# A transformer block on one core: early loads on one queue, the first tile of x in halves, a shorter warm-up

## The chip, the cores and the metric

The kernel runs on one core of a Trainium2 chip. Such a core has a matrix engine (TensorE, PE in the profile, with its weight loads shown as PEld), a vector engine (VectorE, DVE), an engine for activations and copies (ScalarE, ACT), a general engine (GpSimd, POOL), and a queue engine (SyncE, SP) that here only issues transfers. Each engine works through its own instructions in order and waits on semaphores for the others. Operands lie in SBUF, products land in PSUM, which has eight banks of 128 x 512 numbers in fp32. The metric is the device time of one launch in microseconds.

## The reference

One transformer block on 2048 positions of width 512, all in fp32:

```python
h  = x + attention(layernorm(x), wqkv, wo)   # 32 heads of 16; position s sees s, s-2, ..., s-14
h2 = h + mlp(layernorm(h), w1, b1, w2, b2)   # 1792 wide, relu squared
# attention: q, k, v = layernorm(x) @ wqkv; logits of 8 positions per query, softmax, weighted sum of v; @ wo
```

## The kernel before

The 2048 positions are 16 tiles of 128 rows. Even and odd positions are kept apart, so that the dilated window of a query is a run of neighbours. TensorE multiplies in a rounded format (F32R); to keep accuracy each operand is split into a high and a low part, and a product is three: high by high, low by high, high by low (`mm3`, L213). The high part is a copy that rounds, on ScalarE (`hi`, L137); the low part is the difference, on VectorE or GpSimd (`lo`, L140).

The stages are these.
- Head (L675 to L722): the identity for transposes is built, x tiles 0 to 3 and the first three sets of wqkv columns are asked for, TensorE runs `WARM` transposes of the identity that nobody reads (L689), and tile 0 of x is prepared.
- First phase, tiles 0 to 3 (L723): 16 steps, four sets of columns (pairs of head groups) by four tiles. While tile t is multiplied by set 0, tile t + 1 is transposed in the middle of that product (`start_T`, L692).
- First phase, tiles 4 to 15 (`first_phase`, L752): two tiles at a time by three blocks of 512 columns. Beside it run attention for what is ready, and near its end the output product and the transposes of the first four tiles for the MLP.
- MLP, four groups of four tiles (L829), with the rest of attention beside the first ones.

q, k and v go out to DRAM and come back as windows. Attention is a stream of VectorE and GpSimd work, handed out bit by bit (`pump`, L405) by planned costs of VectorE and TensorE; chores with due times are kept in `due` and `late` (L99). All of this only decides, while the program is written, in which order the instructions stand on each engine.

Preparing a tile of x takes: the load; its statistics on VectorE (`norm_stats`, L145: L149 and L150); on GpSimd an addition and a power for one over the root of the variance (L155, L157); the normalisation on VectorE, in place (L187); four transposes on TensorE into a PSUM bank (L196); the high part on ScalarE, the low part on VectorE (both shown as L138 and L141, tiles xh and xl). A set of weights comes in four blocks of 128 rows; each is loaded (wraw), its high part goes to big_h on ScalarE, its low part to big_l.

PSUM banks are given out by turns. A turn counts its tiles and takes the next bank of its list; whoever takes a bank waits until what was in it has been read:

```python
turn = {"mm": Turn("mm0", "mm1"), "tr": Turn("tr0", "tr1")}            # L134
turn["mm"] = Turn("mm0", "mm1", "acc0", "acc1")                        # L447, first phase
turn["tr"] = turn["mm"] = Turn("mm0", "mm1")                           # L828, MLP
```

A `Turn` adds one to its count before it takes a bank, so a new one starts with its second bank. In the first phase "mm" serves the products and the transposes for the MLP (`h_T`, L606), "tr" the warm-up and the other transposes. ScalarE empties a product's bank a step later (`evac`, L483, the copy at L489).

Early in the kernel before, x 0 and x 1, two weight blocks of set 0, x 2, x 3 and all further sets are issued by the sync queue, and the first two blocks of set 0 by ScalarE's queue. VectorE's order at the head is: statistics of tile 0, of tile 1, normalisation of tile 0, low part of block 0, normalisation of tile 1, low part of tile 0, low part of block 1, statistics of tile 2. GpSimd's: L155 and L157 for tile 0, for tile 1, the fills of `zero` and `mask`, low parts of blocks 2 and 3, then L155 and L157 for tile 2. ScalarE copies the four high parts of the weights and then that of tile 0.

Of the kernel before, what the change touches and what calls it, by code (L numbers as in the profile page):

```python
# [9 lines left out]
F32R = mybir.dt.float32r  # L10
AF = mybir.ActivationFunctionType
ALU = mybir.AluOpType
X = mybir.AxisListType.X

S, D, H, DH, W, F = 2048, 512, 32, 16, 8, 1792
P = 128
KB = D // P
# [25 lines left out]
UP = 14, 14, 15, 15  # L43
HOLD = 1.0
XS = 6
WARM = 24


@with_exitstack
def block_kernel(ctx, tc, x, wqkv, wo, w1, b1, w2, b2, out):  # L50
    nc = tc.nc
# [26 lines left out]
    ident = const.tile([P, P], F32, name="ident")  # L78
# [14 lines left out]
    def row(name, shape=(P, D), dt=F32):  # L93
        return work.tile(list(shape), dt, name=name, tag="row", bufs=ROWS)
# [4 lines left out]
    due = {}  # L99
    late = {}  # L100
    now = {"slot": 0, "pe": 0.0, "dve": 0.0, "sub": -1}

    def at(delta, fn, *a):
        due.setdefault(now["slot"] + delta, []).append((fn, a))

    def after(delta, fn, *a):
        late.setdefault(now["slot"] + delta, []).append((fn, a))
# [8 lines left out]
    def run(chores):  # L116
        todo = chores.get(now["slot"], [])
        while todo:
            fn, a = todo.pop(0)
            fn(*a)  # L120

    def dve(t):
        now["dve"] += t
# [10 lines left out]
    turn = {"mm": Turn("mm0", "mm1"), "tr": Turn("tr0", "tr1")}  # L134


    def hi(dst, src):  # L137
        nc.scalar.copy(dst, src)  # L138

    def lo(eng, dst, src, h):  # L140
        eng.tensor_tensor(out=dst, in0=src, in1=h, op=ALU.subtract)  # L141

    stats = {}

    def norm_stats(key, src, delay=True):  # L145
        st = small.tile([P, 6], F32, name="st")
        mv = small.tile([P, 2], F32, name="mv", bufs=4)
        rs = small.tile([P, 2], F32, name="rs", bufs=4)
        nc.vector.bn_stats(st, src)  # L149
        nc.vector.bn_aggr(mv, st)  # L150
        dve(0.93)
        stats[key] = mv, rs

        def finish():
            nc.gpsimd.tensor_scalar(out=rs[:, 1:2], in0=mv[:, 1:2], scalar1=EPS, scalar2=None,  # L155
                                    op0=ALU.add)
            nc.gpsimd.tensor_tensor(out=rs[:, 0:1], in0=rs[:, 1:2], in1=mhalf, op=ALU.pow)  # L157
            if delay:
                nc.gpsimd.tensor_scalar(out=rs[:, 1:2], in0=mv[:, 0:1], scalar1=rs[:, 0:1],
                                        scalar2=-1.0, op0=ALU.mult, op1=ALU.mult)  # L160
        if delay:
            after(0, finish)
        else:
            finish()

    def act_stats(key, src):

        nm = small.tile([P, 2], F32, name="nm", bufs=3)
        sq = small.tile([P, 1], F32, name="sq", bufs=3)
        rs = small.tile([P, 2], F32, name="rs", bufs=4)  # L170
        scrap = row("scrap")
        nc.scalar.activation(scrap, src, AF.Identity, accum_out=nm[:, 0:1])
        nc.scalar.activation(nm[:, 1:2], nm[:, 0:1], AF.Identity, scale=-1.0 / D)
        nc.scalar.activation(scrap, src, AF.Square, bias=nm[:, 1:2], accum_out=sq)
        stats[key] = nm, rs

        def finish():
            nc.gpsimd.tensor_scalar(out=rs[:, 1:2], in0=sq, scalar1=1.0 / D, scalar2=EPS,
                                    op0=ALU.mult, op1=ALU.add)
            nc.gpsimd.tensor_tensor(out=rs[:, 0:1], in0=rs[:, 1:2], in1=mhalf, op=ALU.pow)  # L180
            nc.gpsimd.tensor_tensor(out=rs[:, 1:2], in0=nm[:, 1:2], in1=rs[:, 0:1], op=ALU.mult)
        after(0, finish)

    def norm_apply(key, dst, src, eng):
        mv, rs = stats.pop(key)
        if eng is nc.vector:
            nc.vector.tensor_scalar(out=dst, in0=src, scalar1=mv[:, 0:1], scalar2=rs[:, 0:1],  # L187
                                    op0=ALU.subtract, op1=ALU.mult)
            dve(0.46)
        else:  # L190
            nc.scalar.activation(dst, src, AF.Identity, scale=rs[:, 0:1], bias=rs[:, 1:2])

    def transposes(src, banks="tr"):
        tr = turn[banks].tile("tr").rearrange("p (k c) -> p k c", k=KB)
        for k in range(KB):
            nc.tensor.transpose(tr[:, k, :], src[:, k * P:(k + 1) * P], ident)  # L196
        now["pe"] += 0.44
        return tr
# [223 lines left out]
    xt, xT = {}, {}  # L422

    def load_x(t):
        b, r = divmod(t, 8)
        e, i = divmod(r, 4)
        xt[t] = row("xt")
        nc.sync.dma_start(xt[t], x_v[b, e, i])

    def x_stats(t):  # L430
        if t < XS:
            norm_stats(t, xt[t], t >= R)
        else:
            act_stats(t, xt[t])

    def x_norm(t):
        norm_apply(t, xt[t], xt[t], nc.scalar if t >= R else nc.vector)

    def x_T(t):
        tr = transposes(xt.pop(t))  # L440
        xT[t] = row("xh", (P, KB, P), F32R), row("xl", (P, KB, P), F32R)
        at(0, hi_T, tr, [xT[t][0]])
        after(0, lo_T, tr, [xT[t][0]], [xT[t][1]])
# [8 lines left out]
    def pair(w, k, gp):  # L452
        return w[:, k].rearrange("p (c n) -> p c n", c=3)[:, :, gp * GP:(gp + 1) * GP]
# [62 lines left out]
    def load_wqkv(gp, ks=range(KB), eng=nc.sync):  # L516
        for k in ks:
            if k % 2 == 0:
                tag = "pr" if (gp, k) in ((1, 2), (2, 0), (2, 2)) else "o"
                raws[gp] = att.tile([P, 2, D], F32, name="wraw", tag=tag, bufs=3)  # L520
            r = raws[gp, k] = raws[gp][:, k % 2, :3 * GP].rearrange("p (c n) -> p c n", c=3)
            src = wqkv[k * P:(k + 1) * P].rearrange("p (c n) -> p c n", c=3)
            eng.dma_start(r, src[:, :, gp * GP:(gp + 1) * GP])

    def hi_wqkv(gp, k):
        hi(pair(wq_h, k, gp), raws[gp, k])

    def lo_wqkv(gp, k, eng=nc.vector):
        lo(eng, pair(wq_l, k, gp), raws.pop((gp, k)), pair(wq_h, k, gp))
        if eng is nc.vector:  # L530
            dve(0.48)
# [144 lines left out]
    nc.gpsimd.memset(mhalf, -0.5)  # L676

    load_x(0)
    load_wqkv(0, (0, 1), nc.scalar)
    load_x(1)  # L680
    load_wqkv(0, (2, 3))
    for x0 in (2, 3):
        load_x(x0)
    load_wqkv(1)
# [3 lines left out]
    warm = turn["tr"].tile("tr").rearrange("p (k c) -> p k c", k=KB)  # L688
    for n in range(WARM):  # L689
        nc.tensor.transpose(warm[:, n % KB, :], ident, ident)  # L690
# [6 lines left out]
    def consts():  # L697
        nc.sync.dma_start(b1_sb, b1.rearrange("(f p) -> p f", p=P))
        nc.sync.dma_start(b2_sb, bass.AP(tensor=b2.tensor, offset=b2.offset, ap=[[0, P], [1, D]]))

    x_stats(0)
    x_stats(1)
    x_norm(0)
    hi_wqkv(0, 0)
    lo_wqkv(0, 0)
    x_norm(1)
    nc.gpsimd.memset(zero, 0.0)
    nc.gpsimd.memset(mask, 0.0)
    nc.gpsimd.affine_select(out=mask, in_=mask, pattern=[[1, R], [1, W]], base=1 - W,
                            channel_multiplier=R, compare_op=ALU.is_ge, fill=NEG)  # L710
    nc.sync.dma_start(chain(0, 0, 0, 0, [[GC, PAD], [CS, 6 * G], [1, GC]]),
                      zero.unsqueeze(1).to_broadcast([PAD, 6 * G, GC]))
    for k in range(1, 4):
        hi_wqkv(0, k)
    x_T(0)
    run(due)
    run(late)
    lo_wqkv(0, 1)
    lo_wqkv(0, 2, nc.gpsimd)
    lo_wqkv(0, 3, nc.gpsimd)  # L720
    x_stats(2)
    now["dve"] = now["pe"] = 0.0  # L722
    for n in range(16):  # L723
# [105 lines left out]
    for u in range(R):  # L829
# [9 lines left out]
        todo, halves = {}, {}  # L839
# [48 lines left out]
    h = hs[S // P - 1]  # L888
# [34 lines left out]
```

## Time and profile before

| | us |
|---|---|
| median of 3 runs | 519.74 |
| lowest and highest | 519.19, 520.53 |
| the profiled execution, whole | 518.92 |
| its span from first to last instruction | 517.1 |
| PE busy | 509.9 (99%) |
| DVE busy | 356.0 (69%) |
| POOL busy | 308.2 (60%) |
| ACT busy | 241.9 (47%) |

The span leaves out what lies around the first and the last instruction, 1.8 us here. A row of the timeline gives the start and the length in us, the engine, the line of the kernel, the operation, what it writes and reads by the program's names, shapes, and how many instructions were merged into the row; in brackets stands for how long the engine had been idle and what released it. A row of the waits gives who waited for whom, the total in us, how often, and the longest. A row of the windows gives the stretch and its length, the busy time of each engine, the granted clock, the busy share of the transfer engines and the GB/s moved. Matmul records overlap, because their ends are modelled; the distance between starts is what tells their rate.

### The profile page before, as it was taken

What the parts mean: (1) busy time and instruction counts of PE and PEld (TensorE: products, weight loads), DVE (VectorE), ACT (ScalarE), POOL (GpSimd) and SP (SyncE); (2) the same over time, 40 slices, a digit from 0 to 9 for tenths busy, and PEclk for the clock granted to TensorE, in tenths of its full rate; (3) what the DMA queues carried; (4) which work ended last, traced back from release to release, by engine and by line L of the source; (5) the groups of instructions that cost most, each with busy time, mean ns of one, the idle gap of its engine ahead of it and who ended that gap; (6) DMA issues with size and microseconds to landing.
All of it is one profiled execution on the core that took longest, in us unless ns stands there. A gap on an engine that the chain in (4) does not pass through costs nothing.

```text
span 517.1 us, 7168 instructions
## 1 busy us (share of the span) xinstructions
PE 509.9 (99%) x2385; PEld 426.1 (82%) x2385; DVE 356.0 (69%) x479; ACT 241.9 (47%) x465; POOL 308.2 (60%) x387
## 2 busy tenths in 40 slices
PE   7999999999999999999999999999999999999997
PEld 7999788888887888877888888888888888888886
DVE  5489899989997898967889789888982015211113
ACT  4635587766425664362364345236434332633340
POOL 4714889894784995796588669767799322000000
PEclk9999999999999999999999999999999999999999
DMA  8677989898767885766387438567630321210312
GB/s 264 200 213 185 293 280 311 270 273 278 238 199 207 268 286 164 205 194 201 120 271 222 145 103 249 186 181 236 194 112 22 122 84 56 105 42 21 106 57 81
DMA packets 80622, 93.67 MB, mean 181 GB/s; under 512 B 7881, under 2 KB 49097, under 8 KB 80585
## 3 DMA queue, kind: packets, MB, share of 16 engines
q1 hardware_dynamic: 79640, 92.70, 58.1%
q10 hardware_dynamic: 944, 0.52, 0.3%
q8 instruction: 18, 0.29, 0.2%
q14 instruction: 20, 0.16, 0.1%
HBM read 68.98 MB, written 24.25 MB: 180 GB/s over the span
## 4 chain that ended last, share of the span: by engine, by line
PE 54%; DMA 1%; POOL 1%; DVE 1%; ACT 0%; issue 0%; POOLq 0%; DVEq 0%
PE acc L642 24%; PE mm L221 23%; PE wo L221 5%; PE tr L196 2%; DMA k<-qkv_d 1%; DVE pr L331 0%; PE half L665 0%; DMA w2l_d<-big_l 0%; POOL pr L399 0%; POOL big_l L141 0%; POOL h L583 0%; POOL rl L141 0%; DVE ex L365 0%; DVE w_x L141 0%; DVE big_l L141 0%
## 5 line engine op out<-in xcount | busy, mean ns | idle before, releaser
L399 POOL TENSOR_TENSOR pr<-pr 128x512 f32<-128x512 f32 (+1 forms) x128 | 132.0, 1031 | 52.4 <-DVE pr L342 47.3
L221 PE MATMUL mm<-big_l,w_h 128*128 128x512 f32 x448 | 119.1, 392 | 0.8 <-DVE ol L141 0.5
L221 PEld LDWEIGHTS mm<-big_l,w_h 128*128 128x128 f32 x448 | 83.3, 188 | 18.7 <-DVE ol L141 0.9
L618 ACT ACTIVATE r<-mm,b_sb 128x512 f32<-128x512 f32 x56 | 38.5, 687 | 96.3 <-PE mm L221 92.3
L331 DVE TENSOR_TENSOR pr<-qp,k 128x1024 f32<-128x1024 f32 x64 | 76.9, 1202 | 8.5 <-ACT qp L260 7.4
L342 DVE TENSOR_TENSOR pr<-ex,v 128x1024 f32<-128x1024 f32 x64 | 78.0, 1221 | 5.3 <-POOL o L399 2.9
L365 DVE TENSOR_REDUCE ex<-pr 128x64 f32<-128x1024 f32 x64 | 78.5, 1226 | 1.9
L141 POOL TENSOR_TENSOR rl<-r,rh 128x512 fp32r<-128x512 f32 x42 | 55.2, 1316 | 26.3 <-ACT rh L138 26.3
L221 PE MATMUL mm<-big_l,w_l 128*128 128x512 f32 x224 | 60.0, 389 | 0.0
L221 PE MATMUL mm<-big_h,xl 128*128 128x512 f32 (+1 forms) x208 | 56.2, 379 | 0.0
L221 PE MATMUL mm<-big_h,xh 128*128 128x512 f32 (+1 forms) x208 | 53.3, 378 | 0.7 <-ACT xh L138 0.7
L642 PE MATMUL acc<-big_l,rh 128*128 128x512 f32 x189 | 52.8, 391 | 0.0
L221 PE MATMUL mm<-big_l,xh 128*128 128x512 f32 (+1 forms) x208 | 52.8, 375 | 0.0
L642 PE MATMUL acc<-big_h,rh 128*128 128x512 f32 x189 | 52.2, 391 | 0.0
L642 PE MATMUL acc<-big_h,rl 128*128 128x512 f32 x189 | 51.9, 390 | 0.0
L221 PEld LDWEIGHTS mm<-big_l,w_l 128*128 128x128 f32 x224 | 42.0, 188 | 9.0
L141 DVE TENSOR_TENSOR rl<-r,rh 128x512 fp32r<-128x512 f32 x14 | 9.7, 692 | 55.9 <-ACT rh L138 55.9
L489 ACT COPY y<-mm 128x512 f32<-128x512 f32 (+1 forms) x52 | 28.6, 555 | 36.9 <-PE mm L221 27.2
L221 PEld LDWEIGHTS mm<-big_h,xh 128*128 128x128 f32 x208 | 37.7, 188 | 7.0 <-ACT xh L138 1.5
L221 PEld LDWEIGHTS mm<-big_l,xh 128*128 128x128 f32 x208 | 38.2, 188 | 6.1 <-POOL big_l L141 0.2
L221 PEld LDWEIGHTS mm<-big_h,xl 128*128 128x128 f32 x208 | 37.2, 188 | 5.5 <-DVE xl L141 0.4
L642 PEld LDWEIGHTS acc<-big_h,rl 128*128 128x128 f32 x189 | 35.5, 188 | 7.5
(95 smaller groups left out, 715.8 us busy)
## 6 DMA issues: line engine op xcount, KB each, us to landing
k<-qkv_d SPq DMA_DIRECT2D x48, 288.0 KB, 2.7
v<-qkv_d SPq DMA_DIRECT2D x48, 288.0 KB, 4.0
qkv_d<-y SPq DMA_DIRECT2D x18, 512.0 KB, 3.4
big_l<-w2l_d SPq DMA_DIRECT2D x24, 256.0 KB, 3.1
xt<-in_A_x_dram SPq DMA_DIRECT2D x16, 256.0 KB, 4.5
q<-qkv_d SPq DMA_DIRECT2D x32, 128.0 KB, 3.0
h<-in_A_x_dram SPq DMA_DIRECT2D x16, 256.0 KB, 3.4
h_d<-h SPq DMA_DIRECT2D x16, 256.0 KB, 4.2
```

The lines of the kernel that those rows point to most:

```text
L141: eng.tensor_tensor(out=dst, in0=src, in1=h, op=ALU.subtract)
L196: nc.tensor.transpose(tr[:, k, :], src[:, k * P:(k + 1) * P], ident)
L221: nc.tensor.matmul(ps, l(k), r(k), start=(n == 0), stop=(n == 3 * KB - 1))
L331: nc.vector.tensor_tensor(out=pr.rearrange("p i w h d -> p i w (h d)"), in0=qps["now"][:, j % 2].unsqueeze(2).to_broadcast([P, RI, W, GC]) ...
L342: nc.vector.tensor_tensor(out=p2, in1=vwin, op=ALU.mult, in0=e1[:, :, :, j * GH:(j + 1) * GH].unsqueeze(4).to_broadcast([P, RI, W, GH, DH]))
L365: nc.vector.tensor_reduce(out=lf[:, :, :, j * GH:(j + 1) * GH], in_=pr, axis=X, op=ALU.add)
L399: nc.gpsimd.tensor_tensor(out=dst, in0=p2[:, :, :w], in1=p2[:, :, w:2 * w], op=ALU.add)
L489: nc.scalar.copy(y[:, :, t % RI * GC:(t % RI + 1) * GC], ps[:, :j * GC].rearrange("p (j c) -> p j c", j=j))
L618: nc.scalar.activation(r, ps, AF.Relu, bias=b1_sb[:, f:f + 1])
L642: nc.tensor.matmul(acc[j], l[:, j * P:(j + 1) * P], w[f], start=(first and n < len(js)), stop=(last and n >= len(terms) - len(js)))
```

## The change

The two weight blocks on ScalarE's queue move to the sync queue, between x 0 and x 1, with a third one; the fourth follows x 1. The warm-up has 19 transposes instead of 24. Tile 0 of x is normalised in two halves of 256 columns, each transposed by two transposes into a bank of its own, taken from the turn "mm" instead of "tr", with a copy (high part) and a difference (low part) for each half. On VectorE the statistics of tile 1 now come behind the two half normalisations, and the low parts of blocks 1 and 3 behind the normalisation of tile 1. On GpSimd the low part of block 0 comes between L157 of tile 0 and L155 of tile 1, that of block 2 behind L157 of tile 1, and the fills of `zero` and `mask` behind that. On ScalarE the high part of block 3 comes behind those of the two halves. From the statistics of tile 2 on, the order on every engine is as before.

```diff
-WARM = 24
+WARM = 19
     load_x(0)
-    load_wqkv(0, (0, 1), nc.scalar)
+    load_wqkv(0, (0, 1, 2))
     load_x(1)
-    load_wqkv(0, (2, 3))
+    load_wqkv(0, (3,))
...
     x_stats(0)
+    mv, rs = stats.pop(0)
+    x_0, xT[0] = xt.pop(0), (row("xh", (P, KB, P), F32R), row("xl", (P, KB, P), F32R))
+    hi_wqkv(0, 0)
+    lo_wqkv(0, 0, nc.gpsimd)
+    hi_wqkv(0, 1)
+    hi_wqkv(0, 2)
+    halves = []
+    for c in range(2):
+        cs = slice(c * D // 2, (c + 1) * D // 2)
+        nc.vector.tensor_scalar(out=x_0[:, cs], in0=x_0[:, cs], scalar1=mv[:, 0:1],
+                                scalar2=rs[:, 0:1], op0=ALU.subtract, op1=ALU.mult)
+        tr = turn["mm"].tile("tr")[:, :D // 2].rearrange("p (k c) -> p k c", k=KB // 2)
+        for k in range(KB // 2):
+            nc.tensor.transpose(tr[:, k], x_0[:, cs][:, k * P:(k + 1) * P], ident)
+        halves.append((tr, *[a[:, c * KB // 2:(c + 1) * KB // 2] for a in xT[0]]))
     x_stats(1)
-    x_norm(0)
-    hi_wqkv(0, 0)
-    lo_wqkv(0, 0)
+    for tr, h, l in halves:
+        hi(h, tr)
+    hi_wqkv(0, 3)
+    for tr, h, l in halves:
+        lo(nc.vector, l, tr, h)
     x_norm(1)
+    lo_wqkv(0, 1)
+    lo_wqkv(0, 2, nc.gpsimd)
+    lo_wqkv(0, 3)
     nc.gpsimd.memset(zero, 0.0)
...
-    for k in range(1, 4):
-        hi_wqkv(0, k)
-    x_T(0)
-    run(due)
-    run(late)
-    lo_wqkv(0, 1)
-    lo_wqkv(0, 2, nc.gpsimd)
-    lo_wqkv(0, 3, nc.gpsimd)
     x_stats(2)
```

## The prediction

> **What bounds the kernel now.** I read the page's busy shares first, then TensorE's waits.
>
> ```profile
> PE 509.9 (99%) x2385; PEld 426.1 (82%) x2385; DVE 356.0 (69%) x479; ACT 241.9 (47%) x465; POOL 308.2 (60%) x387
> ```
>
> ```profile
> core 0 of [0], span 517.1 us
> PE tr L690 <- POOL mhalf L676: 1.3, 1, 1.3
> PE mm L221 <- ACT xh L138: 0.7, 1, 0.7
> PE tr L196 <- DVE xt L187: 0.6, 1, 0.6
> PE tr L196 <- ACT y L489: 0.4, 1, 0.4
> PE mm L221 <- ACT r L618: 0.3, 1, 0.3
> PE mm L221 <- DVE ol L141: 0.5, 1, 0.5
> ```
>
> TensorE is busy 509.9 of 517.1 us. So a microsecond won or lost anywhere on its path is a microsecond of the kernel, unless a later wait swallows it, and the waits are few: 1.3 us before the warm-up, 0.7 and 0.6 around the first tile, and three of 0.3 to 0.5 later. The change can win at most about the 1.3 us of the two head waits plus what the first tile's chain is shortened by. I therefore read the head by engine, in the timeline (start, length, engine, line). VectorE:
>
> ```profile
> 4.11 0.69 DVE L149 BATCH_NORM_STATS2 st<-xt 128x6 f32<-128x512 f32 x1 [4.11 <-DMA xt<-in_A_x_dram]
> ...
> 5.40 0.70 DVE L149 BATCH_NORM_STATS2 st<-xt 128x6 f32<-128x512 f32 x1 [0.39 <-DMA xt<-in_A_x_dram]
> ...
> 6.23 0.52 DVE L187 TENSOR_SCALAR xt<-xt,mv,rs 128x512 f32<-128x512 f32 x1
> ...
> 7.68 0.55 DVE L187 TENSOR_SCALAR xt<-xt,mv,rs 128x512 f32<-128x512 f32 x1 [0.47 <-POOL rs L157]
> ...
> 8.75 0.99 DVE L141 TENSOR_TENSOR big_l<-wraw,big_h 128x384 fp32r<-128x384 f32 x1
> ...
> 14.36 0.80 DVE L187 TENSOR_SCALAR xt<-xt,mv,rs 128x512 f32<-128x512 f32 x1
> ```
>
> GpSimd:
>
> ```profile
> 5.41 0.57 POOL L157 TENSOR_TENSOR rs<-rs,mhalf 128x1 f32<-128x1 f32 x1
> ```
> ```profile
> 8.30 1.02 POOL L141 TENSOR_TENSOR big_l<-wraw,big_h 128x384 fp32r<-128x384 f32 x1
> ```
> ```profile
> 6.91 0.74 POOL L157 TENSOR_TENSOR rs<-rs,mhalf 128x1 f32<-128x1 f32 x1
> ```
> ```profile
> 13.32 0.57 POOL L157 TENSOR_TENSOR rs<-rs,mhalf 128x1 f32<-128x1 f32 x1
> 13.86 1.02 POOL L141 TENSOR_TENSOR big_l<-wraw,big_h 128x384 fp32r<-128x384 f32 x1
> ```
>
> TensorE:
>
> ```profile
> 1.61 2.77 PE L690 MATMUL tr<-ident 128*128 128x128 f32 x12
> ...
> 5.24 0.94 PE L690 MATMUL tr<-ident 128*128 128x128 f32 x6
> 6.81 0.66 PE L196 MATMUL tr<-ident,xt 128*128 128x128 f32 x4 [0.62 <-DVE xt L187]
> 8.14 0.97 PE L221 MATMUL mm<-big_h,xh 128*128 128x384 f32 x4 [0.67 <-ACT xh L138]
> ...
> 9.69 0.60 PE L196 MATMUL tr<-ident,xt 128*128 128x128 f32 x4
> ...
> 12.50 0.60 PE L196 MATMUL tr<-ident,xt 128*128 128x128 f32 x4
> ...
> 15.32 0.62 PE L196 MATMUL tr<-ident,xt 128*128 128x128 f32 x4
> ```
>
> Two things are to be seen. The first products of tile 0 start at 8.14. And VectorE and GpSimd hold each other up: the normalisation takes 0.55 us at 7.68, with no subtraction of weights beside it, but 0.80 when it is issued at 14.36 inside a GpSimd subtraction of weights that runs from 13.86 to 14.88; it ends 0.28 us after that subtraction does (15.16). The VectorE subtraction at 8.75 ends at 9.74, 0.42 us after GpSimd's of 8.30 ended (9.32). Whoever comes second waits until the first is through.
>
> **The change, part by part.** *Loads.* The two weight loads leave ScalarE's queue, and the sync queue issues x 0, three weight blocks, x 1, the fourth block, x 2, x 3. How much earlier x 0 lands isn't shown; I bound it.
>
> ```profile
> 1.50:3.00 1.50, 1.50 (x8) 1.50 (x9) 0.00 (x0) 0.94 (x1) 0.00 (x0) 1.00 0.67 162
> ```
>
> By 3.0 us 243 KB had been moved (1.5 us at 162 GB/s); a tile of x is 262 KB. [...] I take 0.7. x 1 is moved behind three weight issues and comes later than 5.40: by bytes, 262 + 590 + 262 KB at about 300 GB/s from there, near 6.1. ScalarE loses two issues, which only brings its table load forward. Behind these eight issues the sync queue stands waiting for a landing now, so later loads keep about their times.
>
> *The head's order on VectorE and GpSimd.* GpSimd's queue is now: the root of tile 0 (L157), the weight subtraction of block 0, the root of tile 1, the subtraction of block 2, then the fills of zero and mask. Behind each root stands a weight subtraction whose inputs have long landed, and each root is also what a normalisation on VectorE waits for. Rows 13.32 and 13.86 show such a pair: the subtraction starts 0.03 us before the root's end (13.89). A normalisation starts 0.03 after its root (7.65 and 7.68). So GpSimd comes first by some 0.06 us and VectorE is shut out for the subtraction's 1.02. Step by step, all from the rows above:
> - root 0 ends 0.7 earlier, 5.98 - 0.7 = 5.28; the subtraction runs 5.25 to 6.27; the first half of the normalisation ends half of the 0.28 later, 6.41, the second some 0.33 later, 6.74. That is where the whole one ends now (6.75). The price of a half isn't shown; between half and all of 0.55 I take 0.41 alone and 0.33 behind its like, since successive instructions there overlap a little (6.23 + 0.52 = 6.75). The 0.7 us of the load are gone.
> - Transposes in two pairs, at 6.47 and 6.80, two copies to xh instead of one, the fourth block's copy behind them: first product near 7.4 instead of 8.14 (1.33 now from the first transpose; two transposes fewer and half the copy make it about 0.9), the fourth, which waits for that last copy, near 8.15. This gains 0.7, for tile 0 alone.
> - The statistics of tile 1 now stand behind the second half: start 6.66 instead of 5.40. Its root ends near 8.53, the subtraction of block 2 runs 8.49 to 9.51, tile 1's normalisation ends 9.51 + 0.28 = 9.80 where it now ends 8.23. Its transposes move from 9.69 to 9.85, and the gain in tile 0 is spent waiting.
> - VectorE still owes two weight subtractions (blocks 1 and 3, 0.55 each when undisturbed) before the statistics of tile 2, which therefore start near 10.7, a microsecond later than now. Chain: 0.70 + 0.2 statistics, 0.9 for the two GpSimd steps, normalisation at 12.57 to 13.11: the transposes of tile 2 go from 12.50 to about 13.17, 0.67 later.
> - Tile 3: statistics to 13.9, root to 14.9, and GpSimd's first subtraction of the next block set (13.86 now) follows at 14.87 to 15.88; the normalisation ends near 16.17 and the transposes go from 15.32 to 16.2. Loss 0.9.
> After tile 3 no normalisation is left in this stage, TensorE is dense, and the 0.9 stays. With x 0 at its old time the same chain loses 0.9 + 0.7 = 1.6. If VectorE came first both times, I get 0.35 by the same steps.
>
> *Warm-up.* Twelve transposes take 2.77 us, 0.213 apart; nineteen end near 5.6, before the data is there (6.47). Five fewer thus gain nothing by themselves, and cost nothing as long as TensorE is at full rate by then; the later ones run faster (four in 0.66). The Trainium skill (TensorE: Matmul & The Clock Gate, What's actually happening) says that the clock opens after a free-running window of about 3.4 us that was busy. By it 19 instead of 24 slow transposes (4.1 us instead of 5.1) leave fewer phases in which a busy window is complete before the idle stretch. In this run the speed-up came during the six from 5.24 on (0.94 us, where 0.213 apart would make 1.3), which the nineteenth, starting at 5.24 too, just reaches. Without this rule the cost is 0; with it, in an unlucky phase, the four transposes and first products run at half rate, some 0.4 us by the rows' 0.213 against 0.11 apart.
>
> *PSUM banks.* The two half tiles are taken from the four-bank turn "mm" instead of "tr". Through the first phase that turn hands out 16 tiles for the pairs, 72 for the column blocks, 4 for wo and 4 for h_T: 96 before, 98 after. A shift within a turn of four changes no distance, but where the turn is replaced (L828) a new one starts with mm1. Before, mm1 was last held by tile 93 (96 is mm0, 95 acc1, 94 acc0). After, it is held by tile 95's place in the old order, the last block of columns before the MLP, which is finished right when the MLP wants its bank.
>
> ```profile
> 163.03 1.09 PE L221 MATMUL mm<-big_l,w_h 128*128 128x512 f32 x4
> ```
> ```profile
> 163.28 0.59 ACT L489 COPY y<-mm 128x512 f32<-128x512 f32 x1 [0.80 <-PE mm L221]
> ```
>
> The MLP's first product starts at 163.03 with no wait; ScalarE empties that last block from 163.28 to 163.87. With 0.05 us to pass it on (xh to first product, as at the head) the product can start at 163.92: 0.89 us lost, on TensorE itself, with all its later work queued behind.
>
> Is either loss swallowed later? The two waits of 0.3 and 0.5 us could return up to 0.8 if VectorE's stream kept its times. But it waits on TensorE in between:
>
> ```profile
> 202.30 0.69 DVE L573 TENSOR_TENSOR h<-wo,h 128x512 f32<-128x512 f32 x1 [1.72 <-PE wo L221]
> ```
>
> With TensorE late, this wait grows by the same amount and the stream moves along. I take nothing back.
>
> **Sum.** The profiled execution took 518.92 us (span 517.1 and 1.8 around it): 518.92 + 0.9 + 0.89 = 520.7. The median of the runs, 519.74, lies 0.82 above the profiled one; the same step gives 521.5.
>
> **Rivals.**
> 1. *VectorE gets through first.* The race for the shared path is won by 0.06 us only. If the normalisations start before the subtractions, the head loses 0.35 instead of 0.9 and the time is about 521.0, which is not slower by the bound used here. It decides at the two roots of tiles 0 and 1. Against it: rows 13.32 and 13.86.
>    The Trainium skill (SBUF — State Buffer, SBUF: two separate sides) has the shared pair go to whoever starts first, for the whole instruction. The rows agree with that (0.80 at 14.36).
> 2. *The bank wait is swallowed.* If the waits of 0.3 and 0.5 absorb it, 520.7. For it: they are on the same engine. Against: the wait at 202.30.
> 3. *The early x doesn't come early*, so the reordered queue doesn't do what it says, or the clock opens late: head 1.3 to 1.6, time 522.2. For it: in the 1.5 us to 3.0 the moved rate was low with little company yet.
> 4. *The head gains outright*: the shut-outs are shorter than read and the 0.7 us of the first product pass through, with the bank wait: 519.9; with luck in both, faster.
>
> **How the numbers follow.** 0.3% is 1.56 us, about what a measurement of this kernel can tell from no change: slower means over 521.30, faster under 518.18. Forecast (both losses, 521.0 to 522.0) 0.54, of which 0.42 lies above 521.30; rival 1 0.15, of which 0.04; rival 2 0.10, of which 0.01; rival 3 0.15, all of it; rival 4 0.06, with 0.04 faster. Slower 0.62, same 0.34, faster 0.04. The range runs from 520.2, below rivals 1 and 2, to 522.6, above rival 3.
>
> **What would show it.** First half of the normalisation ending with GpSimd's subtraction, not 0.3 us after the root; tile 1's statistics at 6.7; transposes of tiles 1, 2, 3 near 9.9, 13.2, 16.2; first products of tile 0 before 7.6; TensorE waiting 0.9 us on ScalarE's copy of y near 164 to 165 where there was no wait. The prediction is wrong if x 0 reaches VectorE at 4.1 or the normalisations aren't blocked, and wrong in its larger certain part if that wait isn't there.

## The result, and the profile after

The changed kernel takes 522.34 us (median of 5 runs, 521.43 to 522.85); the kernel before beside it 519.68 (519.19 to 520.53). The ratio is 1.0041, 95% interval 1.0022 to 1.0059: 0.4% slower, 2.7 us at the medians where 1.8 were forecast. The profiled execution of the changed kernel took 522.34 us (span 520.5), 3.42 more than that of before, so its trace shows somewhat more loss than the medians (2.7 us).

The head, from the timeline of the changed kernel (start, length, engine, line, operation); TensorE:

```profile
6.66 0.76 PE L716 MATMUL tr<-ident,xt 128*128 128x128 f32 x4 [1.00 <-DVE xt L712]
7.56 0.79 PE L221 MATMUL mm<-big_h,xh 128*128 128x384 f32 x3
9.25 0.69 PE L221 MATMUL mm<-big_h,xh 128*128 128x384 f32 x1 [0.89 <-ACT big_h L138]
9.73 1.48 PE L221 MATMUL mm<-big_h,xl 128*128 128x384 f32 x4
11.01 1.06 PE L196 MATMUL tr<-ident,xt 128*128 128x128 f32 x4
...
14.29 0.60 PE L196 MATMUL tr<-ident,xt 128*128 128x128 f32 x4
...
17.10 0.60 PE L196 MATMUL tr<-ident,xt 128*128 128x128 f32 x4
```

VectorE, and below it GpSimd:

```profile
3.62 0.69 DVE L149 BATCH_NORM_STATS2 st<-xt 128x6 f32<-128x512 f32 x1 [3.62 <-DMA xt<-in_A_x_dram]
...
5.53 1.08 DVE L712 TENSOR_SCALAR xt<-xt,mv,rs 128x256 f32<-128x256 f32 x1 [1.00 <-POOL rs L157]
...
7.38 0.69 DVE L149 BATCH_NORM_STATS2 st<-xt 128x6 f32<-128x512 f32 x1 [0.45 <-DMA xt<-in_A_x_dram]
...
9.30 1.22 DVE L187 TENSOR_SCALAR xt<-xt,mv,rs 128x512 f32<-128x512 f32 x1 [0.37 <-POOL rs L157]
10.44 1.02 DVE L141 TENSOR_TENSOR big_l<-wraw,big_h 128x384 fp32r<-128x384 f32 x2
11.38 0.68 DVE L149 BATCH_NORM_STATS2 st<-xt 128x6 f32<-128x512 f32 x1
```
```profile
5.46 0.99 POOL L141 TENSOR_TENSOR big_l<-wraw,big_h 128x384 fp32r<-128x384 f32 x1
...
9.23 1.00 POOL L141 TENSOR_TENSOR big_l<-wraw,big_h 128x384 fp32r<-128x384 f32 x1
```

Five things are to be seen. Tile 0 is earlier (first transposes 6.66 instead of 6.81, first product 7.56 instead of 8.14). Tiles 1, 2 and 3 are later, 11.01, 14.29 and 17.10 instead of 9.69, 12.50 and 15.32. Both times GpSimd's subtraction starts just before the normalisation (5.46 and 5.53; 9.23 and 9.30), and the normalisation takes until after it (the first half 1.08; tile 1's whole 1.22 instead of 0.55). The statistics of tile 1 wait for x 1, at 7.38. And the fourth product waits 0.89 us for the copy of the fourth weight block, which lands late too. The statistics of tile 2 come at 11.38 instead of 9.66 (the row below is from before); that number will matter.

```profile
9.66 0.68 DVE L149 BATCH_NORM_STATS2 st<-xt 128x6 f32<-128x512 f32 x1
```

The loads, from the windows of one microsecond (window, busy time of TensorE, granted clock, share of the transfer engines, GB/s), first of before, then after:

```profile
6.00:7.00 1.00, 0.38 (x4) 1.00 1.12 395
7.00:8.00 1.00, 0.46 (x4) 1.00 1.05 367
```
```profile
6.00:7.00 1.00, 0.34 (x3) 1.00 0.86 249
7.00:8.00 1.00, 0.85 (x5) 1.00 0.87 235
...
9.00:10.00 1.00, 0.75 (x2) 0.59 1.10 325
...
12.00:13.00 1.00, 1.00 (x6) 0.71 1.05 314
```

With all issues on one queue 235 to 249 GB/s move where 367 to 395 did. And TensorE, which had been at full rate (three products in 0.79 us at 7.56), is put back to half rate from 9.18 to 12.58 (0.59 of the window 9 to 10 means 0.82 us at half; 0.71 of 12 to 13 means 0.58), which the products at 9.73 show (1.48 us for four).

The second loss is where the MLP begins (timeline of the changed kernel):

```profile
166.31 1.20 PE L221 MATMUL mm<-big_l,w_h 128*128 128x512 f32 x4 [0.73 <-ACT y L489]
```
```profile
165.67 0.59 ACT L489 COPY y<-mm 128x512 f32<-128x512 f32 x1 [0.80 <-PE mm L221]
```

This copy runs 2.39 us later than in before (163.28), the product 3.28 later (163.03): the wait put 0.89 us on top. The rest of the profile difference, 2.39 less the 1.78 of the head, arises between 46 and 95 us, in a few short waits that this execution has and that of before hasn't:

```profile
PE tr L196 <- ACT xt L191: 0.2, 1, 0.2
PE mm L221 <- DVE xl L141: 0.2, 1, 0.2
```

The profile of before with only the banks moved (below) shows waits of the second kind too, 0.8 us in all, so I do not count them to the change; why they come and go isn't settled.

### The profile page after: what moved, and what is told of

It reads as the page before. It is cut to its first block, busy times and chain, and to the rows that moved or that the text cites. A ratio compares the mean times of both kernels' runs of the same rounds, so it can differ in the third digit from the quotient of the medians.

```text
span 520.5 us, 7164 instructions
## 1 busy us (share of the span) xinstructions
PE 511.5 (98%) x2380; PEld 426.9 (82%) x2380; DVE 357.0 (69%) x481; ACT 242.2 (47%) x466; POOL 308.0 (59%) x387
## 4 chain that ended last, share of the span: by engine, by line
PE 53%; DVE 2%; DMA 2%; POOL 1%; ACT 0%; issue 0%; DVEq 0%
PE acc L642 24%; PE mm L221 23%; PE wo L221 5%; PE tr L196 2%; DMA k<-qkv_d 2%; DVE pr L331 1%; PE half L665 0%; POOL big_l L141 0%; POOL h L583 0%; DVE ex L365 0%; DVE pr L342 0%; DVE w_x L141 0%; DVE big_l L141 0%; ACT r L618 0%; ACT r L619 0%
```

## The experiments

All ratios are to the kernel before, run on the same chip in turn; that kernel took 520.06 us at the median beside the first four, 519.21 beside the next four, 519.00 beside the last four. My theory at the start: the order on VectorE and GpSimd cost the head 0.9 us or more, the bank wait 0.9. The rivals: the loads, late for x 1, or the clock, or the halves as such.

### The banks

The changed kernel with the turn moved two places on, and the kernel before with the same:

```diff
+    turn["mm"].n += 2
     x_stats(1)
```
```diff
+    turn["mm"].n += 2
     x_stats(0)
```

> The changed kernel with two more counts of the product turn behind the half tiles, so that the turn is shifted by four, that is not at all, and everything else stays. Bank theory: the 0.73 us wait of TensorE on ScalarE's copy of y at the first MLP product goes, and 0.9 to 1.0 us come back: about 521.4. Rival (the head alone makes the loss, the bank wait only takes the place of a later one): about 522.3, with some 0.8 us of new waits near 231 and 240 us.

> The kernel before with two extra counts of the product turn at the head and nothing else. Bank theory: a wait of about 0.7 us on ScalarE's copy of y appears at the first MLP product near 163 us, the head is as before, and the time is 519.7 + 0.9 = 520.6. Rival (swallowed later): 519.7.

Measured: 521.77 us, ratio 1.0028 (1.0014 to 1.0042), for the first; 520.87, ratio 1.0013 (1.0003 to 1.0024), for the second. The first products of the MLP, in the timelines of the one and the other:

```profile
166.00 1.07 PE L221 MATMUL mm<-big_l,w_h 128*128 128x512 f32 x4
```
```profile
165.77 1.19 PE L221 MATMUL mm<-big_l,w_h 128*128 128x512 f32 x4 [0.73 <-ACT y L489]
```

The wait goes with the turn, in both kernels, and costs some 0.7 us by the second ratio (0.2 to 1.2 by its interval). That is the one part whose price holds by itself. The first run's ratio is 0.7 us below the changed kernel's own, with intervals that overlap, and its edit does one thing more: two places on, the first product of tile 0 gets the bank in which the first half still stands, and waits until VectorE has made its low part. It starts at 8.59 instead of 7.56:

```profile
8.59 1.65 PE L221 MATMUL mm<-big_h,xh 128*128 128x384 f32 x4 [1.17 <-DVE xl L141]
```

That run's profile also had its clock put back for longer, to which I come below; whether this wait caused it isn't shown.

### The loads

The changed kernel with the loads of before, and the kernel before with the changed loads:

```diff
-    load_wqkv(0, (0, 1, 2))
+    load_wqkv(0, (0, 1), nc.scalar)
     load_x(1)
-    load_wqkv(0, (3,))
+    load_wqkv(0, (2, 3))
```
```diff
-    load_wqkv(0, (0, 1), nc.scalar)
+    load_wqkv(0, (0, 1, 2))
     load_x(1)
-    load_wqkv(0, (2, 3))
+    load_wqkv(0, (3,))
```

> The changed kernel with the loads of before (two weight blocks on ScalarE's queue). Order theory (normalisation shut out behind GpSimd's weight subtraction, statistics of tile 1 behind the halves): x 0 lands at 4.1 again, the root of tile 0 at 6.0, halves end at 7.1 and 7.5, statistics of tile 1 start near 7.4 as in the changed kernel, so the transposes of tile 3 stay near 17 us and the time near 522.2. Load theory (x 1 landing at 7.35 and weight block 3 at 8.66 make the loss and, through TensorE's idle time, the half clock from 9 to 12.5 us): the transposes of tile 3 come back to 16.2 or before, the clock holds, and the time is 521.4 or less.

> The kernel before with only the loads of the changed one. Here the statistics of tile 1 stand in front of the normalisation of tile 0 on VectorE. Load theory: x 1 lands at 7.4, so the normalisation of tile 0 starts at 8.3 instead of 6.2, and the whole head is 1.5 to 2 us later: 521.2 to 521.7. Order theory (the loads are harmless by themselves, x 1 near 6.1): at most 0.5 us: 519.7 to 520.2.

Measured: 522.32 us, ratio 1.0044 (1.0029 to 1.0060), with the loads put back; 523.34, ratio 1.0060 (1.0038 to 1.0082), with the loads alone. From their timelines, the first kernel and then the second:

```profile
9.02 1.22 DVE L187 TENSOR_SCALAR xt<-xt,mv,rs 128x512 f32<-128x512 f32 x1 [0.37 <-POOL rs L157]
```
```profile
6.86 0.69 DVE L149 BATCH_NORM_STATS2 st<-xt 128x6 f32<-128x512 f32 x1 [2.31 <-DMA xt<-in_A_x_dram]
```

The loads alone harm the old order most, by more than the 521.2 to 521.7 expected: there the statistics of tile 1 stand ahead of the normalisation of tile 0, and both wait for x 1 (VectorE idles 2.31 us). That is not all of its loss: its profile is 1.8 us longer than that of before by the span (518.9), and five of its six executions, the profiled one excepted, show a mean clock of 0.993 to 0.997, although the warm-up has 24 transposes. So the clock seems to be lost with late data too; no trace shows it. In the changed order nothing is gained by taking them back: x 1 is early then, but its statistics stand behind the halves (7.11), x 0 is 0.26 later, and the time is the same. So the late x 1 is a cost of the loads that the changed order hides, and the changed order has its own price of the same size.

### GpSimd's subtractions and the order

First, on top of the loads put back, no subtraction of GpSimd just ahead of a normalisation; then the changed order alone, with loads, warm-up and banks as in before.

```diff
     hi_wqkv(0, 0)
-    lo_wqkv(0, 0, nc.gpsimd)
     hi_wqkv(0, 1)
     hi_wqkv(0, 2)
+    lo_wqkv(0, 2, nc.gpsimd)
...
+    lo_wqkv(0, 0)
     x_stats(1)
...
     lo_wqkv(0, 1)
-    lo_wqkv(0, 2, nc.gpsimd)
     lo_wqkv(0, 3)
```
```diff
-WARM = 19
+WARM = 24
...
+    turn["mm"].n += 2
     x_stats(1)
```

> The changed kernel with the early loads of before, in which the weight subtraction of block 0 runs on VectorE behind the two halves, and that of block 2 on GpSimd ahead of the second root, so that no subtraction of GpSimd starts just before a normalisation. In the run with the loads alone put back the first half took 1.08 us and the normalisation of tile 1 1.22, against 0.40 for the second half and 0.52 to 0.55 in before. Theory (GpSimd's 0.99 us subtraction, released by the same root, holds VectorE's normalisation up): the halves take about 0.4 us each and the normalisation of tile 1 about 0.55; the transposes of tile 1 start about 0.65 earlier than the 10.29 there, at 9.6 to 9.8, and those of tile 3 near 16.1 instead of 16.76; the kernel stays 1.3 to 1.8 us over before, for the bank wait of 0.73 is still there and tile 1's statistics still stand behind the halves. Rival (the stretch is the price of half a width or of the pointers, or of the moment): 1.0 to 1.2 us stay, and tile 1 starts at 10.3 again.

> The halves and the new order of the head alone: loads and warm-up of before, and two turns more of the banks so that the MLP finds them as in before. With the loads put back but the short warm-up and the bank wait in, the transposes of tile 3 started at 16.76 in the profile, 1.44 later than in before. Theory: the transposes of tiles 1 to 3 at 10.2, 13.6 and 16.7, the kernel 1.2 to 1.5 us over before, with little spread; the normalisation of tile 1 takes 1.2 us. Rival (the order itself is harmless, the short warm-up is what cost it): transposes of tile 3 at 15.3 to 15.8 and at most 0.5 over before.

Measured: 520.93 us, ratio 1.0035 (1.0023 to 1.0047), and 520.86 us, ratio 1.0033 (1.0021 to 1.0045). VectorE and one row of TensorE in the first, then the same in the second:

```profile
5.99 0.73 DVE L712 TENSOR_SCALAR xt<-xt,mv,rs 128x256 f32<-128x256 f32 x2 [1.00 <-POOL rs L157]
...
9.02 0.55 DVE L187 TENSOR_SCALAR xt<-xt,mv,rs 128x512 f32<-128x512 f32 x1 [0.38 <-POOL rs L157]
```
```profile
7.61 1.65 PE L221 MATMUL mm<-big_h,xh 128*128 128x384 f32 x4
```
```profile
5.91 1.40 DVE L712 TENSOR_SCALAR xt<-xt,mv,rs 128x256 f32<-128x256 f32 x2 [1.00 <-POOL rs L157]
...
9.14 1.36 DVE L187 TENSOR_SCALAR xt<-xt,mv,rs 128x512 f32<-128x512 f32 x1 [0.37 <-POOL rs L157]
```
```profile
8.50 0.97 PE L221 MATMUL mm<-big_h,xh 128*128 128x384 f32 x4 [0.69 <-DVE xl L141]
```

With no subtraction of GpSimd beside them the same halves take 0.41 each and the normalisation 0.55: the stretch was the shut-out. Tile 3 starts at 16.15 there, 0.61 earlier than with the loads alone put back, as expected; tile 1 doesn't (10.33), since TensorE was still at half rate in that execution (1.65 us for four products). By the ratios, 1.0035 against 1.0044, the shut-out's price isn't resolved: their intervals overlap. The order alone costs 1.7 us by its ratio, somewhat more than the 1.2 to 1.5 expected, and its tile 3 starts at 17.01, 1.69 late. That is the largest single part. Its edit too makes the first product wait for its bank (0.69 us, at 8.50), but the transposes of tile 1 wait behind that for their normalisation all the same (0.40 us, at 10.56), so the bank isn't what sets them.

### The warm-up

The changed kernel with `WARM = 24`, twice, the second time beside the unchanged changed kernel on one chip; and the kernel before with `WARM = 19`.

> The changed kernel with 24 warm-up transposes instead of 19: the warm-up ends near 6.2 us instead of 5.66, still before the first transposes of x at 6.66. In the changed kernel TensorE fell back to half rate from 9.2 to 12.6, after gaps of 1.00 and 0.89 us. Theory A (the shorter warm-up left the gap that cost the clock): no fall, products 0.18 apart throughout, transposes of tile 1 near 10.2 instead of 11.01 and of tile 3 near 16.4 instead of 17.10: 0.5 to 0.8 us faster than the changed kernel. Theory B (the gap of 0.89 at the late third block costs the clock, whatever the warm-up): the fall stays, and the time with it, within 0.2 us of the changed kernel.

> The kernel before with 19 warm-up transposes and nothing else changed. The prediction costed this at nothing: the clock of the profile of before rose at 5.5 us, and the gap before the first transposes of x grows from 0.62 to about 1.1 us. Theory A (nothing): within 0.15 us of before, transposes of tiles 0 to 3 at 6.8, 9.7, 12.5 and 15.3. Rival B (the longer gap costs the clock, so that some executions fall back to half rate): 0.3 to 0.8 us slower, with products 0.32 apart somewhere between 8 and 13 us.

> The changed kernel as it is, on one chip with the two runs below, so that they can be set against each other: about 1.004 times before by its own runs. In some of its executions the mean clock is 0.993 to 0.997, in others 0.999 to 1.000.

> The changed kernel with 24 warm-up transposes, beside the changed kernel on the same chip. In before, the shorter warm-up alone cost 1.25 us at the median and left 9 of 12 executions with a lower mean clock or over 522. Theory A (the costs add up): 0.8 to 1.3 us faster than the changed kernel. Theory B (in the changed kernel the first products wait for the fourth weight block and for the normalisation of tile 1 anyway, so that half rate lies beside those waits): the mean clock is 0.999 to 1.000 throughout, but the time is within 0.5 us of the changed kernel.

Measured, with the mean granted clock that each execution shows:

```
                                  median   ratio (95%)               clock 0.997 or less
before, WARM 19                   520.55   1.0024 (1.0009 to 1.0040)   7 of 12 executions
before, WARM 24, same group       519.21                               0 of 23
changed, WARM 24, second group    521.75   1.0050 (1.0036 to 1.0064)   0 of 6
changed, as it is, last group     521.99   1.0048 (1.0036 to 1.0060)   2 of 6
changed, WARM 24, last group      521.44   1.0047 (1.0035 to 1.0059)   0 of 5
```

In the kernel before the shorter warm-up alone costs 1.3 us at the median, which the prediction had at nothing. Three of the twelve executions lost nothing (518.68 to 519.45); the profiled one was among these, so no trace shows this kernel's loss. Two took 522.8 and 522.9 with a mean clock of 1.000. The changed kernel as it is shows in its second profile how a late clock can look under that number:

```profile
6.74 1.11 PE L716 MATMUL tr<-ident,xt 128*128 128x128 f32 x4 [1.08 <-DVE xt L712]
...
10.63 1.48 PE L221 MATMUL mm<-big_h,xl 128*128 128x384 f32 x4
...
14.04 0.91 PE L221 MATMUL mm<-big_h,xh 128*128 128x384 f32 x4
```

Its rate never rose during the warm-up; all ran at half rate until near 14 us, while the clock column reads 1.00. Whether the two executions of 522.8 are of this kind I infer from that and haven't seen. In the changed kernel 24 transposes keep the clock, but the time gains only 0.55 us at the medians on one chip (intervals overlap): nearer to theory B. TensorE waits there anyway, 0.50 us for the fourth block and 0.81 for the normalisation of tile 1 (the waits of TensorE, in the last run, then a row from the first run with 24):

```profile
PE tr L196 <- DVE xt L187: 0.8, 1, 0.8
...
PE mm L221 <- ACT big_h L138: 0.5, 1, 0.5
```
```profile
9.90 0.44 PE L221 MATMUL mm<-big_h,xh 128*128 128x384 f32 x1 [1.57 <-ACT big_h L138]
```

In that first run the clock held as theory A had it, but the rest of theory A fell: the fourth block came later still, the transposes of tiles 1 and 3 started at 11.11 and 17.57 instead of 10.2 and 16.4, and the ratio shows no gain.

### The halves with all else put right

First with the statistics of tile 1 ahead of the halves, and loads, warm-up, banks and most subtractions as in before; then with the normalisation of tile 1 ahead of the subtractions of xl, and block 3 moved from GpSimd to VectorE. The first diff is against the changed kernel, the second against the first; the old places of the subtractions and the lines for loads, warm-up and banks are left out.

```diff
     x_stats(0)
+    x_stats(1)
...
-    x_stats(1)
+    lo_wqkv(0, 0)
     for tr, h, l in halves:
         hi(h, tr)
...
+    lo_wqkv(0, 1)
+    lo_wqkv(0, 2, nc.gpsimd)
+    lo_wqkv(0, 3, nc.gpsimd)
```
```diff
     lo_wqkv(0, 0)
+    x_norm(1)
...
-    x_norm(1)
...
     lo_wqkv(0, 1)
+    lo_wqkv(0, 3)
     lo_wqkv(0, 2, nc.gpsimd)
-    lo_wqkv(0, 3, nc.gpsimd)
```

> The halves alone, with what went against them taken away: the loads of before, 24 warm-up transposes, the statistics of tile 1 ahead of the halves as before, the subtraction of block 0 on VectorE and the others in the places they have in before, and two turns more of the banks, so that the first products of the MLP find the banks that they find in before. Theory (halves as such gain, since the first product no longer waits for a copy of the whole tile): first half at 6.2 to 6.6, first product at 7.4 to 7.6 instead of 8.14, transposes of tile 1 at 8.9 to 9.3 instead of 9.69, of tile 2 near 12.1 (held by its normalisation, which stood at 11.56 in before) and of tile 3 near 15.0: 0.2 to 0.5 us faster than before. Rival (what the head waits for is later than tile 0: statistics of tiles 2 and 3): transposes of tiles 2 and 3 at 12.4 to 12.6 and 15.2 to 15.4 as in before, and no difference.

> The reworked head of the last run (halves, statistics of tile 1 ahead of them, loads, warm-up and banks as in before), with two moves more. There the normalisation of tile 1 took 1.35 us beside GpSimd's subtraction from 8.20, and VectorE's subtraction of block 1 1.35 more. Here the normalisation stands ahead of the two subtractions of xl on VectorE, and only block 2 is left to GpSimd. Theory (what is left of the loss is VectorE shut out): the normalisation of tile 1 starts near 7.8 and takes 0.55, the transposes of tiles 1, 2 and 3 start near 9.2, 12.0 and 14.9 (9.69, 12.50 and 15.32 in before), and the kernel is 0.3 to 0.5 us faster than before. Rival (the subtraction of block 2 shuts out another instruction instead, and statistics of tile 2 come late again): transposes of tile 3 at 15.6 or later, no gain or a loss.

Measured: 520.15 us, ratio 1.0020 (1.0010 to 1.0029), and 520.03, ratio 1.0018 (1.0009 to 1.0027). Neither beats the kernel before, though the first products start at 7.48 and 7.55 and TensorE's waits around tile 0 are nearly gone. Both expectations of a gain fell. VectorE in the first, where GpSimd's subtractions run from 8.20 to 10.35, and then in the second, with its GpSimd and TensorE rows below:

```profile
8.13 1.35 DVE L187 TENSOR_SCALAR xt<-xt,mv,rs 128x512 f32<-128x512 f32 x1
9.41 1.35 DVE L141 TENSOR_TENSOR big_l<-wraw,big_h 128x384 fp32r<-128x384 f32 x1
```
```profile
10.26 0.68 DVE L149 BATCH_NORM_STATS2 st<-xt 128x6 f32<-128x512 f32 x1
...
12.16 0.55 DVE L187 TENSOR_SCALAR xt<-xt,mv,rs 128x512 f32<-128x512 f32 x1 [0.43 <-POOL rs L157]
12.62 0.69 DVE L149 BATCH_NORM_STATS2 st<-xt 128x6 f32<-128x512 f32 x1
...
14.75 1.01 DVE L187 TENSOR_SCALAR xt<-xt,mv,rs 128x512 f32<-128x512 f32 x1
```
```profile
14.46 4.11 POOL L141 TENSOR_TENSOR big_l<-wraw,big_h 128x384 fp32r<-128x384 f32 x4
```
```profile
14.97 0.90 PE L221 MATMUL mm<-big_h,xl 128*128 128x384 f32 x4
15.91 0.63 PE L196 MATMUL tr<-ident,xt 128*128 128x128 f32 x4
```

Here a chain beside tile 0 sets the end of the head: statistics of tile 2, its root and normalisation, statistics of tile 3, its root, and then GpSimd's next subtraction (14.46) shuts the normalisation of tile 3 out until 15.76; its transposes follow at 15.91, 0.94 us after the group of products ahead of them began. In before they follow that group after 0.74 (to the 15.32 of the prediction's rows), as the transposes of tile 1 do, which wait for nothing (8.95 to 9.69):

```profile
14.58 0.90 PE L221 MATMUL mm<-big_h,xl 128*128 128x384 f32 x4
```

So there TensorE comes to them by itself, just as the normalisation (until 15.16) lets it go: two chains end together. Over the fourteen profiles (start of two steps, in us; "banks only", "GpSimd kept clear", "changed, loads put back" and all "changed" but "banks back" have the bank wait in their ratio as well):

```
                                     statistics   transposes
                                     of tile 2    of tile 3    difference   ratio
before                                  9.66        15.32        5.66
before, WARM 19                         9.64        15.29        5.65       1.0024
banks only                              9.61        15.27        5.66       1.0013
halves, normalisation first            10.26        15.91        5.65       1.0018
halves, rest put right                 10.69        16.34        5.65       1.0020
GpSimd kept clear                      10.44        16.15        5.71       1.0035
changed, loads put back                11.11        16.76        5.65       1.0044
loads only                             11.11        16.77        5.66       1.0060
order alone                            11.37        17.01        5.64       1.0033
changed                                11.38        17.10        5.72       1.0041
changed, WARM 24                       11.93        17.57        5.64       1.0050
changed, WARM 24, again                11.58        17.23        5.65       1.0047
changed, banks back (late clock)       11.46        18.34        6.88       1.0028
changed, again (late clock)            11.25        18.30        7.05       1.0048
```

In twelve of fourteen, tile 3 starts 5.64 to 5.72 us after the statistics of tile 2, whatever was done to tile 0. The two others are the profiles with long half rate. In six of the twelve (both with the halves, loads put back, order alone, both with 24 transposes) the normalisation of tile 2 waits for its root, and tile 3's transposes come 0.93 to 1.00 us after the group ahead of them: VectorE's chain is the later one. In the other six, before and the changed kernel among them, they follow after 0.72 to 0.74, so TensorE's own chain is the later one, but by less than 0.1 us if VectorE's takes 5.65 there too. In the changed kernel TensorE's is so late because of the fourth block and the half rate; with 24 transposes the rate holds, and tile 3 is no earlier, since VectorE's chain is as late. So the head loses at least what VectorE is late by at the statistics of tile 2, and the clock adds to it only where half rate lasts long enough to become the later of the two. A version that starts those statistics before 9.66 and the first product before 8.14 should gain; this wasn't tried.

## Why the prediction was right, and where it was not

*The sign and the range* hold: 522.34 lies in 520.2 to 522.6, and the forecast was slower, with two losses, both of which came. But it lies above the forecast's own band, 521.0 to 522.0: the head lost 1.78 us instead of 0.9. The range reaches 522.6 for the sake of rival 3, so that it holds is in part luck. Rival 4, a gain, falls with the sign.

*The bank wait* holds with its size: 0.89 forecast, 0.89 in the profile (0.73 shown as waiting; the rest is how far a product's modelled record overlaps the next one where nothing waits), and not swallowed: the turn alone costs 0.7 by its ratio. Rival 2 falls, though the interval of that ratio leaves room for a part of it.

*The race for the shared path* holds. GpSimd came first by 0.07 us both times, and VectorE ended 0.16 and 0.29 us behind the subtraction; 0.28 was forecast for the second, and half of it for a half. Rival 1 falls. The Trainium skill (SBUF — State Buffer, SBUF: two separate sides) has whoever starts first hold the pair for the whole instruction; the runs agree, 1.22 us beside GpSimd and 0.55 without.

*The early x* came 0.49 us earlier: 3.62 instead of 4.11. No run shows the 0.7 that the forecast took, and root 0 ended at 5.50 (forecast 5.28). The fourth product came at 9.25, not 8.15, since the fourth weight block landed later than I assumed.

*The step that failed is the landing of x 1.* I put it "near 6.1" by bytes "at about 300 GB/s", and so hidden behind the halves; the statistics of tile 1 would start at 6.66. The row shows 7.38, released by the landing. The statistics of tile 2 followed at 11.38 instead of "near 10.7", and tile 3 at 17.10 instead of 16.2: of the 0.9 us by which the head was forecast too short, 0.7 are this term. What the forecast left out is the time that the queue spends on issuing. The rows of the sync queue's issues, first of before (both tiles of x), then of the changed kernel (three weight blocks, x 1):

```profile
0.73 0.87 SPq L428 DMA_DIRECT2D xt<-in_A_x_dram  x2
```
```profile
1.18 1.98 SPq L523 DMA_DIRECT2D wraw<-in_A_wqkv_dram  x3
...
3.19 0.61 SPq L428 DMA_DIRECT2D xt<-in_A_x_dram  x1
```

In before x 1 is issued by 1.60 and used at 5.40, 3.8 us later; here it is issued by 3.80, behind 1.98 us of weight issues, and used at 7.38, 3.6 us later. Rival 3 ("head 1.3 to 1.6") is the nearest to what came in size (1.78), though x 0 did come early; its other condition, a clock that opens late, is what the second profile of the changed kernel shows. But this term isn't the cause of the loss: with the loads put back the time is the same.

*The warm-up* "costs nothing": wrong as a statement on the part, 1.3 us in the kernel before. In the changed kernel it is about 0.5, not clear of noise. The rule that I set beside it, the free-running window of about 3.4 us (the Trainium skill, TensorE: Matmul & The Clock Gate, What's actually happening), pointed the right way, and my price for it, 0.4, left out that the clock may also fall back. The trace agrees with its length: 9.18 to 12.58 is 3.40 us. The profile of the changed kernel with its banks put back shows two such lengths, from 7.54 to 14.36, by the same reading of its windows:

```profile
7.00:8.00 1.00, 0.43 (x3) 0.77 0.91 319
...
14.00:15.00 1.00, 1.00 (x6) 0.82 0.62 148
```

*The parts do not add up neatly.* By the experiments, order 1.7, banks 0.7, warm-up 0.5 and loads about 0 make 2.9; the changed kernel lost 2.1 and 2.5 by its two ratios, 2.7 and 3.0 by the medians. The difference is within their intervals.

## What to carry to other kernels

A wait seen on the busiest engine at the start isn't a gain to be had until the chain behind it is known: here the fourth tile's normalisation, on another engine and seven microseconds later, set the same end, and every edit to the first tile that pushed it back was paid in full there. Before work is handed to a helper engine, look at what releases it: if the same event releases an instruction that shares a path with it, the order of two starts 0.07 us apart costs a whole instruction. And a warm-up that ends early can leave the rate to chance: with 0.62 us between its end and tile 0's transposes (by the profile) none of 23 executions showed a lower clock, with 1.13 us 7 of 12 did.

## What the runs showed of the hardware that I had not expected

- The granted clock can be taken back after gaps of 1.00 and 0.89 us in TensorE's work within 3.6 us, and returns only 3.4 or 6.8 us later (6.8 in the kernel with its banks put back, whose gaps were 1.70 and 1.17). The gaps alone don't decide: with 24 transposes the changed kernel kept its clock through 0.61 and 1.57 us.
- A rate that never rose isn't seen in the clock column: it read 1.00 while products of 384 columns stood 0.32 us apart instead of 0.175. The spacing of like rows tells.
- Issuing eight loads from one queue instead of two lowered what moved in 6 to 8 us to 249 and 235 GB/s; with the two queues back in the same kernel it was 390 and 367 (windows of the kernel with the loads put back):

```profile
6.00:7.00 1.00, 0.08 (x1) 1.00 1.08 390
7.00:8.00 1.00, 0.86 (x5) 1.00 1.07 367
```
